# Computing the shift of an adaptive layer norm with four 128x32 column tiles of TensorE and a VectorE transpose

## The chip, the cores and the metric

The kernel runs on one core of a Trainium2 chip. The metric is the device time of one execution in microseconds; a kernel's time is the median of several executions. TensorE multiplies matrices (its stationary operand is loaded by a separate instruction, shown as PEld), VectorE (DVE) and ScalarE (ACT) do element-wise work, GpSimd (POOL) does a few reductions and small operations, and SyncE (SP) issues nearly all DMA transfers.

## The reference, cut to what matters

```python
B, N, D = (2, 256, 1152)          # all inputs bfloat16

def reference(x, c, wqkv, wo, w_mod):
    mod = (_silu(c) @ w_mod).reshape(B, 6, 1, D)
    shift_a, scale_a, gate_a, ... = [mod[:, i] for i in range(6)]
    h = _layernorm(x, axis=-1) * (1 + scale_a) + shift_a
    qkv = h @ wqkv                 # split into q, k, v of D columns each
    p = _softmax(jnp.einsum('bqd,bkd->bqk', q, k) * D ** (-0.5), axis=-1)
    a = jnp.einsum('bqk,bkd->bqd', p, v) @ wo
    return x + gate_a * a
```

Each batch has one shift, one scale and one gate vector of 1152 values. They are products of `_silu(c)`, a matrix of 2 rows, with slices of `w_mod`.

## The kernel before, in words

The 512 tokens of both batches form one token axis (T = 512). The 1152 features are KT = 9 slices of 128. Nearly everything is kept with features on the partitions and tokens along the free axis, so that `xnT`, `hTs` and `hT` are tiles of 128 x 9 x 512.

Every instruction goes through a small recorder (class `_Rec`, line 65), and at the end `pin` ties the instructions of each engine to the order in which the program wrote them. So the order of the source lines is the order on every engine. Because of the recorder the profile gives line 74 for nearly all instructions, and groups are told apart by the names of their tiles.

The stages are, in order of time:

1. Loads, statistics of the layer norm, transposition of the centred x into `xnT`, and the scale vectors (`psS0`, `psSA`, `psM`, `psL`), which become `s1p` = 1 + scale.
2. The K projection without shift: `hTs` = `xnT` x `s1p`, and accumulation over the nine feature slices. Six of the nine blocks of 128 K columns are accumulated side by side in six PSUM banks (`accs`, NACC = 6). Of the next two (NEARLY = 2) the first KA = 3 slices are computed early and put into the SBUF tile `early`; the other six slices follow later in `k_block`, and VectorE adds the two parts into `qkT`. The ninth block comes last. (A shift of K adds the same number to all scores of a query, which the softmax takes out, and so K does without it.)
3. The shift. `shift_block(kk)` (lines 312 to 317) issues nine matmuls for the kk-th part of the contraction. Their stationary operand is a 128x128 block of `wH`, the shift's slice of `w_mod`. Their moving operand is `sc_rhs(kk)`: silu(c) for both batches, repeated to NR = 54 columns. The result has features on the partitions; `psH` is 128 x 9 x 54, of which two columns of each slice are copied to `sh`. On TensorE four such groups of nine stand ahead of the blocks 6 and 7 of K, one between them, and four behind. The last K block follows (lines 472 to 475).
4. `modulated(i)` computes `hT` = `xnT` x `s1p` + `sh` for 18 pieces (nine slices, two batches); every third goes to ScalarE, the others to VectorE.
5. Nine q blocks of nine matmuls each (lines 510 to 518) read `hT` slice by slice, from `chunks_w`, and ScalarE evacuates them into `qkT`. Then come the scores, the softmax, the value blocks, the products with the probabilities and the output projection. While TensorE does the q blocks, VectorE accumulates the gate vectors (`gacc`), 18 steps of 1152 columns.

PSUM has six banks that rotate (pool `psum`, tag `mm`) and two single ones (`psum_a`, tag `pa`; `psum_b`, tag `pb`). In SBUF the pools lie one behind the other in the order in which they are opened: `const` (small tiles, `sh` among them), `wpool` (`wK` and the q and v weights), `act`, `small`, `work`, and later `wmpool` (`wS`, `wH`).

All loads are issued by SyncE in the order of the program; `wH` is loaded in five parts behind the K weights, and the first q weights follow.

Of the kernel before, what the change touches and what calls it, by code (L numbers as in the profile page):

```python
# [8 lines left out]
ALU = mybir.AluOpType  # L9
AX = mybir.AxisListType  # L10
F32 = mybir.dt.float32
BF16 = mybir.dt.bfloat16
# [4 lines left out]
def kernel(  # L17
# [10 lines left out]
    P = 128  # L28
    B, N, D = x.shape
    T = B * N  # L30
    KT = D // P
    TT = T // P
    NQ = N // P
    CW = 384
# [4 lines left out]
    NACC = 6  # L39
    NEARLY = 2  # L40
    WE = (NACC + NEARLY) * P
    KA = 3
    KM = 2 * KA
    NR = 54
# [4 lines left out]
    wmod_v = w_mod.rearrange("(p kk) (s n) -> p kk s n", p=P, s=6)  # L49
    wo_v = wo.rearrange("(k p) n -> p k n", p=P)  # L50

    const = ctx.enter_context(tc.tile_pool(name="const", bufs=1))
    wpool = ctx.enter_context(tc.tile_pool(name="wpool", bufs=1))
    act = ctx.enter_context(tc.tile_pool(name="act", bufs=1))
    small = ctx.enter_context(tc.tile_pool(name="small", bufs=4))
    work = ctx.enter_context(tc.tile_pool(name="work", bufs=2))
    psum = ctx.enter_context(tc.tile_pool(name="psum", bufs=6, space=PSUM))
    psum_a = ctx.enter_context(tc.tile_pool(name="psum_a", bufs=1, space=PSUM))
    psum_b = ctx.enter_context(tc.tile_pool(name="psum_b", bufs=1, space=PSUM))
# [21 lines left out]
    vec = _Rec(nc.vector, dve_seq)  # L81
    sca = _Rec(nc.scalar, act_seq)
    ten = _Rec(nc.tensor, pe_seq)
# [12 lines left out]
    def tok(b):  # L96
        return slice(b * N, (b + 1) * N)
# [4 lines left out]
        out=ident, in_=ident, compare_op=ALU.not_equal, fill=1.0, base=0,  # L102
# [14 lines left out]
        out=pick, in_=pick, compare_op=ALU.is_ge, fill=0.0, base=0,  # L117
# [3 lines left out]
        out=pick, in_=pick, compare_op=ALU.is_ge, fill=0.0, base=NT - 1,  # L121
# [10 lines left out]
    wK = wpool.tile([P, KT, D], BF16)  # L132
    chunk_cols = [vc * CW for vc in range(NCH)] + [2 * D + vc * CW for vc in range(NCH)]
    chunks_w = [wpool.tile([P, KT, CW], BF16, tag=f"wchunk{i}", name="wqv") for i in range(2 * NCH)]
    wmpool = ctx.enter_context(tc.tile_pool(name="wmpool", bufs=1))
    wS = wmpool.tile([P, KT, D], BF16, tag="wS")
    wH = wmpool.tile([P, KT, D], BF16, tag="wH")

# [62 lines left out]
    def sc_rhs(kk):  # L201
        return scT_rep[:, kk].rearrange("p r b -> p (r b)")
# [5 lines left out]
    hT = act.tile([P, KT, T], BF16)  # L208
# [62 lines left out]
    def rstd_spread():  # L271
# [4 lines left out]


    s1p = const.tile([P, KT, B], F32)
    sh = const.tile([P, KT, B], F32)
    hTs = act.tile([P, KT, T], BF16, tag="a3")  # L280
    qkT = act.tile([P, 2 * KT, T], BF16)
    early = const.tile([P, NEARLY, T], F32)
# [3 lines left out]
               rhs=ones_row[0:1, 0 : (KA - 1) * NR], start=True, stop=False, skip_group_check=True)  # L286
    psS0 = psum_b.tile([P, NR], F32, tag="pb")
    ten.matmul(psS0, lhsT=ones_bf[0:1, :], rhs=ones_row[0:1, 0:NR], start=True, stop=False,
               skip_group_check=True)
# [19 lines left out]
            for b in range(B):  # L309
                scaled(k, tok(b), s1p[:, k, b : b + 1])  # L310

    def shift_block(kk):
        for j in range(KT):
            ten.matmul(
                psH[:, j, :], lhsT=wH[:, kk, j * P : (j + 1) * P], rhs=sc_rhs(kk),
                start=(kk == 0 and j == 0), stop=(kk == KT - 1), skip_group_check=True,
            )

    def one(t):
# [26 lines left out]
    def k_block(f, ps, k0):  # L346
        for k in range(k0, KT):
            ten.matmul(
                ps, lhsT=wK[:, k, f * P : (f + 1) * P], rhs=hTs[:, k, :],
                start=(k == k0), stop=(k == KT - 1),  # L350
            )

    def evac(idx, out_ap, in_ap):
        if idx % 2 == 0:
            return vec.tensor_copy(out=out_ap, in_=in_ap)
        return sca.copy(out=out_ap, in_=in_ap)
# [100 lines left out]
        k_step(k)  # L457
    for f in range(NACC):
        evac(1, qkT[:, KT + f, :], accs[f])
    psH = psum_a.tile([P, KT, NR], F32, tag="pa")  # L460
    for kk in range(4):
        shift_block(kk)
    for i in range(NEARLY):
        pool, tag = (psum_b, "pb") if i == 0 else (psum, "mm")
        ps = pool.tile([P, T], F32, tag=tag, name="ps")
        k_block(NACC + i, ps, KA)
        vec.tensor_tensor(out=qkT[:, KT + NACC + i, :], in0=ps, in1=early[:, i, :], op=ALU.add)
        shift_block(4 + i)
    for kk in range(4 + NEARLY, KT):
        shift_block(kk)  # L470
    vec.tensor_copy(out=sh, in_=psH[:, :, 0:B])
    for f in range(NACC + NEARLY, KT):
        ps = psum.tile([P, T], F32, tag="mm")
        k_block(f, ps, 0)
# [2 lines left out]
    def modulated(i):  # L477
        k, b = divmod(i, B)
        if i % 3 == 2:
            sca.activation(  # L480
                out=hT[:, k, tok(b)], in_=xnT[:, k, tok(b)], func=ACT.Identity,
                bias=sh[:, k, b : b + 1], scale=s1p[:, k, b : b + 1],
            )
        else:
            vec.tensor_scalar(
                out=hT[:, k, tok(b)], in0=xnT[:, k, tok(b)],
                scalar1=s1p[:, k, b : b + 1], scalar2=sh[:, k, b : b + 1],
                op0=ALU.mult, op1=ALU.add,
            )

    for i in range(KT * B):
        modulated(i)
    evac(1, qkT[:, 2 * KT - 1, :], last_k)


# [11 lines left out]
        spq.dma_start(out=wO[:, k0 : k0 + 3, :], in_=wo_v[:, k0 : k0 + 3, :])  # L507


    for f in range(KT):  # L510
        wt, off = chunks_w[f * P // CW], f * P % CW
        ps = psum.tile([P, T], F32, tag="mm")
        for k in range(KT):
            ten.matmul(
                ps, lhsT=wt[:, k, off : off + P], rhs=hT[:, k, :],
                start=(k == 0), stop=(k == KT - 1),
            )
        evac(1, qkT[:, f, :], ps)


    s_tiles = []
    for b in range(B):
        s_ps = psum.tile([P, NQ, N], F32, tag="mm")
        for i in range(NQ):
            tq = b * NQ + i
            for k in range(KT):
                ten.matmul(
                    s_ps[:, i, :],
                    lhsT=qkT[:, k, tq * P : (tq + 1) * P],
                    rhs=qkT[:, KT + k, tok(b)],  # L530
                    start=(k == 0), stop=(k == KT - 1),
# [96 lines left out]
    for b in range(B):  # L628
        for gi, dv0 in enumerate(range(0, KT, 2)):
            ndv = min(2, KT - dv0)  # L630
            ps = psum.tile([P, 2, N], F32, tag="mm")
            for dd in range(ndv):
                dv = dv0 + dd
                for j in range(NQ):
                    ten.matmul(
                        ps[:, dd, :], lhsT=v_sb[:, b * NQ + j, dv * P : (dv + 1) * P], rhs=pT_sbs[b][:, j, :],
                        start=(j == 0), stop=(j == NQ - 1),
# [3 lines left out]
    for t in range(TT):  # L641
# [9 lines left out]
        for ci, (c0, w_) in enumerate(chunks):  # L651
# [3 lines left out]
            ps = psum.tile([P, w_], F32, tag="mm")  # L655
            if pregated:
                ten.matmul(ps, lhsT=ident, rhs=x_sb[:, t, cs], start=True, stop=False)
            for k in range(KT):
                ten.matmul(
                    ps, lhsT=attnT[:, k, t * P : (t + 1) * P],  # L660
                    rhs=(wo_last[:, k, c0 - (D - TAILW) : c0 - (D - TAILW) + w_] if pregated else wO[:, k, cs]),
                    start=(k == 0 and not pregated), stop=(k == KT - 1),
# [49 lines left out]
```

## Time and profile before

| | us |
|---|---|
| median of 3 runs | 97.81 (97.72 to 98.03) |
| the profiled execution, its own time | 98.07 |
| its span, first to last instruction | 96.2 |
| TensorE busy | 90.3 |
| VectorE busy | 70.4 |
| ScalarE busy | 33.7 |
| the 81 shift matmuls, first to last start | 26.1 to 30.8 |

The span is what the views of the trace show; the time around it (98.07 - 96.2 = 1.87 us) lies before the first and behind the last instruction. A timeline line gives start, length, engine, operation, output and inputs, the number of instructions merged, and in brackets the idle time before them with what ended it. Matmuls overlap: the length of one is its latency, and the distance between two starts is what a stream of them costs. The granted clock of TensorE was 1.000 over the whole span.

### The profile page before, as it was taken

What the parts mean: (1) busy time and instruction counts of PE and PEld (TensorE: products, weight loads), DVE (VectorE), ACT (ScalarE), POOL (GpSimd) and SP (SyncE); (2) the same over time, 40 slices, a digit from 0 to 9 for tenths busy, and PEclk for the clock granted to TensorE, in tenths of its full rate; (3) what the DMA queues carried; (4) which work ended last, traced back from release to release, by engine and by line L of the source; (5) the groups of instructions that cost most, each with busy time, mean ns of one, the idle gap of its engine ahead of it and who ended that gap; (6) DMA issues with size and microseconds to landing.
All of it is one profiled execution on the core that took longest, in us unless ns stands there. A gap on an engine that the chain in (4) does not pass through costs nothing.

```text
span 96.2 us, 1820 instructions
## 1 busy us (share of the span) xinstructions
PE 90.3 (94%) x722; PEld 55.4 (58%) x727; DVE 70.4 (73%) x138; ACT 33.7 (35%) x68; POOL 21.4 (22%) x26
## 2 busy tenths in 40 slices
PE   5968799999999999999999999999999999999980
PEld 1338599553566444444448756665568756665670
DVE  0398669224999999999992999991228677998880
ACT  5198577201570972342222436332115400000010
POOL 6600000820000000000000000007999980016000
PEclk9999999999999999999999999999999999999999
DMA  1999999999999999999999502110000000303131
GB/s 33 332 357 372 324 384 376 397 393 416 390 378 396 384 410 387 374 373 372 387 410 408 201 0 48 37 24 0 0 0 0 7 0 0 123 0 123 67 120 58
DMA packets 19015, 21.31 MB, mean 221 GB/s; under 512 B 2752, under 2 KB 13632, under 8 KB 19008
## 3 DMA queue, kind: packets, MB, share of 16 engines
q1 hardware_dynamic: 18592, 21.16, 61.3%
q10 hardware_dynamic: 416, 0.05, 0.3%
q8 instruction: 5, 0.08, 0.3%
q14 instruction: 2, 0.02, 0.0%
HBM read 19.76 MB, written 1.18 MB: 218 GB/s over the span
## 4 chain that ended last, share of the span: by engine, by line
PE 84%; DMA 10%; SPq 2%; issue 1%; DVE 1%; ACT 0%
PE ps L74 63%; PE acc L74 11%; DMA wK<-in_wqkv_dram 5%; DMA wS<-in_w_mod_dram 4%; PE s_ps L74 4%; PE psH L74 2%; SPq L74 2%; PE psE L74 1%; PE psL L74 1%; PE tp L74 1%; DVE xnT L74 0%; PE spread_ps L74 0%; DVE hTs L74 0%; ACT o_sb L74 0%; PE turn_ps L74 0%
## 5 line engine op out<-in xcount | busy, mean ns | idle before, releaser
L74 POOL PARTITION_ALL_REDUCE gate_bc<-gacc x2 | 13.7, 6886 | 45.5 <-DVE gacc L74 45.5
L74 DVE SCALAR_TENSOR_TENSOR gacc<-wG,scT_f,gacc 128x1152 f32<-128x1152 bf16 x16 | 22.7, 1418 | 0.5
L74 PE MATMUL ps<-wqv,hT 128*128 128x384 bf16 x108 | 17.7, 326 | 0.0
L74 PE MATMUL ps<-hT,wqv 128*128 128x512 bf16 x80 | 17.6, 379 | 0.1
L74 PE MATMUL ps<-wO,attnT 128*128 128x384 bf16 (+1 forms) x108 | 17.0, 319 | 0.0
L74 PEld LDWEIGHTS <-attnT 128*128 128x128 bf16 x126 | 11.4, 98 | 6.3
L74 PEld LDWEIGHTS <-hT 128*128 128x128 bf16 x108 | 10.6, 98 | 6.9
L74 PE MATMUL acc<-hTs,wK 128*128 128x128 bf16 (+2 forms) x88 | 13.2, 292 | 1.1 <-DMA wK<-in_wqkv_dram 0.6
L74 PEld LDWEIGHTS <-wK 128*128 128x128 bf16 x123 | 9.9, 97 | 6.8 <-DMA wK<-in_wqkv_dram 0.9
L74 PEld LDWEIGHTS <-wqv 128*128 128x128 bf16 x81 | 7.9, 98 | 9.6 <-DVE hT L74 0.4
L74 ACT CAST qkT<-ps 128x512 bf16<-128x512 f32 x10 | 5.8, 583 | 10.9 <-PE ps L74 10.9
L74 DVE TENSOR_TENSOR ga<-ps,gate_bc 128x384 f32<-128x384 f32 (+1 forms) x12 | 6.5, 538 | 2.7 <-PE ps L74 2.7
L74 ACT CAST v_sb<-ps 128x384 bf16<-128x384 f32 x10 | 4.7, 476 | 9.8 <-PE ps L74 9.8
L74 DVE TENSOR_TENSOR o_sb<-ga,x_sb 128x384 bf16<-128x384 f32 (+1 forms) x12 | 6.8, 565 | 0.4
L74 DVE TENSOR_TENSOR xnT<-xnT,rstd_bc 128x512 bf16<-128x512 bf16 x9 | 5.5, 686 | 1.6 <-ACT rstd_bc L74 1.6
L74 ACT CAST o_sb<-ps 128x128 bf16<-128x128 f32 (+1 forms) x2 | 0.5, 238 | 17.0 <-PE ps L74 17.0
L74 PE MATMUL junk_ps<-junk_rhs 128*128 128x512 bf16 x13 | 4.7, 540 | 1.1 <-DVE junk_rhs L74 1.1
L74 DVE BATCH_NORM_STATS2 stats<-x_sb 128x6 f32<-128x384 bf16 x6 | 3.1, 551 | 2.8 <-DMA x_sb<-in_x_dram 2.8
L74 PE MATMUL ps<-hTs,wK 128*128 128x512 bf16 x19 | 4.7, 378 | 0.1
L74 DVE CAST attnT<-ps 128x512 bf16<-128x512 f32 (+1 forms) x6 | 3.5, 603 | 1.7 <-PE ps L74 1.7
L74 DVE CAST v_sb<-ps 128x384 bf16<-128x384 f32 x2 | 1.1, 558 | 4.6 <-PE ps L74 4.6
L74 DVE TENSOR_SCALAR hTs<-xnT,s1p 128x256 bf16<-128x256 bf16 (+1 forms) x20 | 4.2, 272 | 0.1
(82 smaller groups left out, 89.8 us busy)
## 6 DMA issues: line engine op xcount, KB each, us to landing
wqv<-in_wqkv_dram SPq DMA_DIRECT2D x5, 864.0 KB, 10.1
wG<-in_w_mod_dram SPq DMA_DIRECT2D x3, 864.0 KB, 9.6
wO<-in_wo_dram SPq DMA_DIRECT2D x3, 864.0 KB, 8.5
wH<-in_w_mod_dram SPq DMA_DIRECT2D x4, 576.0 KB, 7.4
wS<-in_w_mod_dram SPq DMA_DIRECT2D x6, 288.0 KB, 6.2
wK<-in_wqkv_dram SPq DMA_DIRECT2D x6, 288.0 KB, 6.4
x_sb<-in_x_dram SPq DMA_DIRECT2D x4, 288.0 KB, 3.6
wqv<-in_wqkv_dram SPq DMA_DIRECT2D x3, 288.0 KB, 8.6
```

The costliest lines, as they stand in the source:

```text
L74: r = fn(*a, **k)
```

## The change

The shift's operands change places. The stationary operand is now 32 columns of silu(c) (16 repetitions of the two batches), the moving operand 288 columns of `wH`: for column group j, columns 32j to 32j + 31 of each of the nine slices. The four groups use the four 128x32 column tiles of TensorE and write partitions 32j to 32j + 31 of `psH`. So 36 matmuls take the place of 81. The result has batches on the partitions; VectorE's transpose of 32x32 blocks turns it, all 288 columns, into `sh`, which is 128 x 9 x 32 now.

The K blocks 6 and 7 run ahead of the shift and stay in their PSUM banks ("parked"); their additions come behind the 18 modulations. The first two q blocks are computed in turns, slice by slice, in two banks.

The pools are opened in another order: a lead tile of 128 bytes, `wpool`, `act`, `wmpool`, `work`, and behind them `const` and `small`.

```diff
-    const = ctx.enter_context(tc.tile_pool(name="const", bufs=1))
+    lead = ctx.enter_context(tc.tile_pool(name="lead", bufs=1))
+    lead.tile([P, 64], BF16, name="lead")
     wpool = ctx.enter_context(tc.tile_pool(name="wpool", bufs=1))
     act = ctx.enter_context(tc.tile_pool(name="act", bufs=1))
+    wmpool = ctx.enter_context(tc.tile_pool(name="wmpool", bufs=1))
+    work = ctx.enter_context(tc.tile_pool(name="work", bufs=2))
+    const = ctx.enter_context(tc.tile_pool(name="const", bufs=1))
     small = ctx.enter_context(tc.tile_pool(name="small", bufs=4))
-    work = ctx.enter_context(tc.tile_pool(name="work", bufs=2))
...
-    sh = const.tile([P, KT, B], F32)
+    sh = const.tile([P, KT, 32], F32)
...
-    def shift_block(kk):
-        for j in range(KT):
+    def shift_rows(kk):
+        w4 = wH[:, kk, :].rearrange("p (f j c) -> p f j c", j=4, c=32)
+        for j in range(4):
             ten.matmul(
-                psH[:, j, :], lhsT=wH[:, kk, j * P : (j + 1) * P], rhs=sc_rhs(kk),
-                start=(kk == 0 and j == 0), stop=(kk == KT - 1), skip_group_check=True,
+                psH[32 * j : 32 * (j + 1), :, :], lhsT=sc_rhs(kk)[:, 0:32], rhs=w4[:, :, j, :],
+                start=(kk == 0), stop=(kk == KT - 1), skip_group_check=True, tile_position=(0, 32 * j),
             )
...
-    psH = psum_a.tile([P, KT, NR], F32, tag="pa")
-    for kk in range(4):
-        shift_block(kk)
+    parked = []
     for i in range(NEARLY):
         pool, tag = (psum_b, "pb") if i == 0 else (psum, "mm")
-        ps = pool.tile([P, T], F32, tag=tag, name="ps")
-        k_block(NACC + i, ps, KA)
-        vec.tensor_tensor(out=qkT[:, KT + NACC + i, :], in0=ps, in1=early[:, i, :], op=ALU.add)
-        shift_block(4 + i)
-    for kk in range(4 + NEARLY, KT):
-        shift_block(kk)
-    vec.tensor_copy(out=sh, in_=psH[:, :, 0:B])
+        parked.append(pool.tile([P, T], F32, tag=tag, name="ps"))
+        k_block(NACC + i, parked[i], KA)
+    psH = psum_a.tile([P, KT, 32], F32, tag="pa")
+    for kk in range(KT):
+        shift_rows(kk)
+    vec.transpose(out=sh.rearrange("p f r -> p (f r)"), in_=psH.rearrange("p f r -> p (f r)"))
...
     for i in range(KT * B):
         modulated(i)
+    for i in range(NEARLY):
+        vec.tensor_tensor(out=qkT[:, KT + NACC + i, :], in0=parked[i], in1=early[:, i, :], op=ALU.add)
     evac(1, qkT[:, 2 * KT - 1, :], last_k)
...
-    for f in range(KT):
-        wt, off = chunks_w[f * P // CW], f * P % CW
-        ps = psum.tile([P, T], F32, tag="mm")
+    for fs in ((0, 1), *((f,) for f in range(2, KT))):
+        pss = [psum.tile([P, T], F32, tag="mm", name="ps") for _ in fs]
         for k in range(KT):
-            ten.matmul(
-                ps, lhsT=wt[:, k, off : off + P], rhs=hT[:, k, :],
-                start=(k == 0), stop=(k == KT - 1),
-            )
-        evac(1, qkT[:, f, :], ps)
+            for f, ps in zip(fs, pss):
+                wt, off = chunks_w[f * P // CW], f * P % CW
+                ten.matmul(
+                    ps, lhsT=wt[:, k, off : off + P], rhs=hT[:, k, :],
+                    start=(k == 0), stop=(k == KT - 1),
+                )
+        for f, ps in zip(fs, pss):
+            evac(1, qkT[:, f, :], ps)
```

More of the change, by code (lines that the diff above doesn't have):

```diff
@@ L134 @@
     chunks_w = [wpool.tile([P, KT, CW], BF16, tag=f"wchunk{i}", name="wqv") for i in range(2 * NCH)]
-    wmpool = ctx.enter_context(tc.tile_pool(name="wmpool", bufs=1))
     wS = wmpool.tile([P, KT, D], BF16, tag="wS")
```

## The prediction

> **What bounds the kernel now.** I read the page first, then the chain of waits in order of time, then the timeline of each engine around the edit, then the transfers' times to landing.
>
> ```profile
> span 96.2 us, 1820 instructions
> PE 90.3 (94%) x722; PEld 55.4 (58%) x727; DVE 70.4 (73%) x138; ACT 33.7 (35%) x68; POOL 21.4 (22%) x26
> ```
>
> TensorE is busy for 94% of the span. The chain says where that sets the end (start, length, what):
>
> ```profile
> 23.61 2.70 PE acc L74 x12
> 26.30 0.91 PE psH L74 x36
> 27.21 0.06 issue
> 27.27 1.24 PE ps L74 x5
> 28.51 0.23 PE psH L74 x9
> 28.73 1.29 PE ps L74 x6
> 30.03 0.91 PE psH L74 x36
> 30.94 0.22 PE ps L74
> 31.16 0.05 issue
> 31.21 10.74 PE ps L74 x49
> ...
> 50.37 3.93 PE s_ps L74 x36
> 54.30 39.17 PE ps L74 x272
> ```
>
> From 23.61 us to the last matmul nothing but TensorE stands in the chain. The shift's 81 matmuls are three of its pieces, so what they cost less, the end moves forward, unless another wait takes the place. The candidates are VectorE and the transfers. VectorE around the edit:
>
> ```profile
> 24.26 5.51 DVE L74 TENSOR_TENSOR xnT<-xnT,rstd_bc 128x512 bf16<-128x512 bf16 x9 [1.56 <-ACT rstd_bc L74]
> 29.69 1.28 DVE L74 TENSOR_TENSOR qkT<-ps,early 128x512 bf16<-128x512 f32 x2
> 30.98 0.18 DVE L74 COPY sh<-psH 128x18 f32<-128x18 f32 x1
> 31.19 3.17 DVE L74 TENSOR_SCALAR hT<-xnT,s1p,sh 128x256 bf16<-128x256 bf16 x12
> 34.28 0.81 DVE L74 TENSOR_SCALAR gacc<-wG,scT_f 128x1152 f32<-128x1152 bf16 x1
> 52.37 0.69 DVE L74 TENSOR_TENSOR p_f<-s_ps,rstd_bc 128x512 f32<-128x512 f32 x1 [2.01 <-PE s_ps L74]
> ```
>
> VectorE runs without a pause from 24.26 us, and has 2.01 us to spare when it reaches the first softmax step at 52.37.
>
> **The change part by part.**
>
> *Removed: 81 matmuls.* The chain's pieces psH are 0.91 + 0.23 + 0.91 = 2.05 us, or 25 ns for each matmul of 54 columns. All of it is on the path.
>
> *Added: 36 matmuls of 288 columns, four beside each other.* The pitch of wide matmuls comes from the timeline: the q blocks start at 32.72 us and the scores at 50.20, with 81 matmuls of 512 columns between, so 17.48 / 81 = 0.2158 us for 512 columns, and 288 columns are 0.1214 us. A step kk has four of them. If the four column tiles stream together, nine steps are 9 x 0.1214 = 1.09 us, and the last of the four starts three issue slots later, 3 x 0.025 = 0.08. If they stream one after another, 36 x 0.1214 = 4.37 us. No row of before shows two column tiles in flight. One row shows one tile of that shape (12 stationary columns, in a tile of 32), with its neighbours:
>
> ```profile
> 21.36 0.38 PE L74 MATMUL acc<-hTs,wK 128*128 128x512 bf16 x1
> 21.67 0.22 PE L74 MATMUL turn_ps<-ident,parts 128*12 128x128 bf16 x1
> 21.82 0.60 PE L74 MATMUL acc<-hTs,wK 128*128 128x512 bf16 x2
> ```
>
> It starts 0.31 us after its predecessor where 0.216 is usual (0.09 lost), and its successor 0.15 us after it where 128 columns need 0.054 (0.10 lost): entering and leaving the narrow tile costs 0.19 us. The new block enters and leaves once.
>
> *Which end I take.* Bounds for the block: below, 36 issue slots of 25 ns, 0.91 us with free edges; above, 4.37 + 0.19 = 4.56 us. I take the concurrent case, 1.09 + 0.08 + 0.19 = 1.36 us. The nearest rows are the psH matmuls themselves: each lasts 185 ns but a new one starts every 25 ns, weight load included, so four loads and starts (0.10 us) fit into one 0.1214 us stream; and the four tiles write different partitions of psH and use different columns of the array. Gain: 2.05 - 1.36 = 0.69 us.
>
> The Trainium skill bears on both halves. "TensorEngine Tiling (Array Packing)", section Key Properties, says a change of tiling mode drains TensorE; the 0.09 and 0.10 us above agree. "TensorE: Matmul & The Clock Gate", Part 3 (Measured speedup vs the span model), gives 2.38 times for three column tiles instead of 3; at that efficiency four would need 4.37 / 3.17 + 0.19 = 1.57 us (an estimate from that page) and the gain would be 0.48 us. No run here shows it yet.
>
> *Moved: the two blocks of K columns 6 and 7 now run ahead of the shift* (12 matmuls, 2.59 us, no change in number). They start at 26.14 us, the block of the shift at 26.14 + 2.59 = 28.73 and K block 8 at 28.73 + 1.36 = 30.09, against 30.78 before (timeline; the chain gives 30.94, the end of the last shift matmul). wH's five transfers were issued from 16.6 to 20.1 us and took 6.7 to 8.5 us, so the last had landed by 28.6: the shift waits for none.
>
> *Evacuation of the shift: COPY of 18 columns (0.18 us) becomes a transpose of 288.* No row is a transpose. Bounds: 0.18 us, and 0.69 us for a 512-column read of PSUM (p_f row); by width between the two, 0.18 + 0.51 x 270 / 494 = 0.46. VectorE is free of the nine multiplications at 29.77, the last shift matmul ends about 30.2, so sh stands at 30.66 and hT starts at 30.70 against 31.19: 0.49 earlier. TensorE reaches the q blocks 1.94 us after 30.09, at 32.03, and the first hT pair is done at 31.3. Even at 0.69 us, or a half microsecond more, the transpose is covered by K block 8.
>
> *q blocks 0 and 1 take turns.* Same 18 matmuls, no cost. Alone, block 0 would want the last slice of hT at 32.03 + 8 x 0.216 = 33.76, when VectorE finishes it (30.70 + 3.17 = 33.87); taking turns it is wanted at 35.48. So it prevents a stall of 0.1 to 0.3 us, and none existed before (80 q matmuls in 17.65 us leave no hole).
>
> *The two additions for K columns 6 and 7 (1.20 us at their spacing, 29.69 to 30.98 less the pause) go behind the modulation.* Queued behind them are the gate's accumulations: these start at 30.70 + 3.08 + 1.20 = 34.98 instead of 34.28, 0.70 later. The eleven others keep their pace (wG's later parts land before they are wanted: issue 26.8 and 30.1, 10.8 and 9.6 us to landing, wanted about 38.7 and 43). VectorE reaches the softmax 0.70 later and TensorE's scores are 0.69 earlier: of the 2.01 us of slack, 0.62 is left. Without that cover the delay would be small still: the value blocks occupy TensorE to 71.7 us while the turned probabilities were there at 63.6. The parked PSUM banks are wanted again only by q block 5.
>
> *Transfers.* No DMA is added or moved. The q weights' second and third parts land at 35.4 and 42.1 (issue 25.7 and 30.9, plus 9.7 and 11.2); q blocks 3 and 6 want them at 37.9 and 43.7, so an earlier TensorE still finds them.
>
> *Pools.* wK starts at byte 40,704 of a partition before and 16,640 after, both multiples of 256; so do all other weight and activation tiles, because the grown sh (1,152 bytes instead of 72) now lies behind them. Small tiles moved from 0 to 32 beyond a multiple of 64. I take nothing for it; the bound is the stretch in which TensorE waits for transfers, 2.65 to 11.94 us: 3% either way would be 0.3 us.
>
> **The sum.** The profiled execution took 98.07 us, of which the span is 96.2: 98.07 - 0.69 = 97.38. It lay 0.26 above the median of the runs; from the median 97.81, 97.12 us.
>
> **Rivals.**
> - *The four tiles stream one after another.* The block is 4.56 us, 2.51 more than before; nothing hides it, as everything behind waits for sh or for TensorE: 97.81 + 2.51 = 100.32 us. It turns slower once the block passes 2.05 us. For it: no row shows two tiles together. Against: different columns and partitions. 0.07.
> - *Weight loads set the pace.* The narrow tile's load took 0.08 us in the trace; four in a row per step are 0.32 us, and 9 x 0.32 + 0.19 = 3.07: +1.02, 98.83 us. For it: each matmul has its own load, and a load after a change of tile was not pulled ahead (0.42 us of idle before it). Against: loads at full width keep to the 25 ns pitch. 0.11. In one sentence from the skill: the Tiling page (Restrictions) says column tiling switches the fast weight load off, which would feed this rival.
> - *Half of the overlap.* Pace 0.2 us a step, through the moving operand's runs of 32 columns out of 128 or loads partly shown: 9 x 0.2 + 0.19 = 2.0, no change, 97.8 us. 0.11.
> - *The wait moves to VectorE* (transpose or additions): covered by the slacks above, so only with a transpose over 1.2 us, 0.02, at about 97.7.
>
> **Chances and range.** Forecast 0.69, the rivals 0.07, 0.11, 0.11 and 0.02. About 0.3% (0.29 us) is what a measurement of this kernel can tell from no change. The forecast's own range is 96.8 (block near 1.1 us) to 97.5 (the estimate with four at the lower efficiency, and the pools); the half overlap reaches 98.2. Faster 0.68, within 0.12, slower 0.20. To leave out no more than 2 in 10 the range goes from 96.6 to 98.3.
>
> **What would show it.** Right: psH matmuls in groups of four starting about 0.12 us apart per step; the block from 28.7 to 30.1; hT from about 30.7; q blocks from 32.0 without a hole; VectorE's wait before p_f about 0.6 us. Wrong: steps of 0.2 us or more, a hole ahead of the q blocks, or a first stage (to 11.9 us) of another length.

## The result and the profile after

The changed kernel takes 97.0 us (median of 15 runs, 96.35 to 98.28), the kernel before 97.81 (15 runs, 97.04 to 98.21). The ratio is 0.9916 with a 95% interval of 0.9886 to 0.9945: faster by 0.8%, or 0.81 us of the medians. The profiled execution of after took 97.0 us, of which 95.2 are the span.

The page of after, its first two parts:

```profile
span 95.2 us, 1731 instructions
PE 90.8 (95%) x678; PEld 54.6 (57%) x682; DVE 70.6 (74%) x138; ACT 33.5 (35%) x68; POOL 21.4 (22%) x26
```

The chain of waits of after (start, length, what):

```profile
23.33 2.69 PE acc L78 x12
26.02 2.59 PE ps L78 x12
28.61 1.22 PE psH L78 x36
29.83 0.32 PE ps L78
30.15 0.05 issue
30.20 10.74 PE ps L78 x49
...
49.36 3.93 PE s_ps L78 x36
53.29 39.17 PE ps L78 x272
```

Three pieces of psH, 2.05 us, have become one of 1.22, and everything behind them is as long as it was: 3.93 us of scores and 39.17 us of the rest in both kernels. VectorE in the timeline of after, from two windows:

```profile
25.80 3.69 DVE L78 TENSOR_TENSOR xnT<-xnT,rstd_bc 128x512 bf16<-128x512 bf16 x6
29.88 0.48 DVE L78 STREAM_TRANSPOSE sh<-psH 128x288 f32<-128x288 f32 x1 [0.40 <-PE psH L78]
30.40 3.16 DVE L78 TENSOR_SCALAR hT<-xnT,s1p,sh 128x256 bf16<-128x256 bf16 x12
33.48 1.28 DVE L78 TENSOR_TENSOR qkT<-ps,early 128x512 bf16<-128x512 f32 x2
34.68 0.81 DVE L78 TENSOR_SCALAR gacc<-wG,scT_f 128x1152 f32<-128x1152 bf16 x1
```
```profile
51.36 0.69 DVE L78 TENSOR_TENSOR p_f<-s_ps,rstd_bc 128x512 f32<-128x512 f32 x1 [0.60 <-PE s_ps L78]
```

The transpose takes 0.48 us where the copy took 0.18, but now VectorE waits 0.40 us for TensorE ahead of it. The slack ahead of the softmax has shrunk from 2.01 to 0.60 us.

**Where to measure.** The stage ahead of the edit is the same code in both kernels, and yet it did not end at the same time: the first matmul behind the six accumulators started at 26.14 us in the profile of before and at 25.86 in that of after. Over the profiles of all kernels below it lies between 25.33 and 26.80 us, without order. So the 1.0 us between the two spans is not all the edit's. What the edit does is read from the *tail*: from the start of the last accumulating matmul plus its pace of 0.216 us, which is where the next one starts in both kernels, to the end of the last matmul. Before: 26.14 to 93.46, 67.32 us. After: 25.86 to 92.45, 66.59 us. The edit is worth 0.73 us there; the 0.81 of the medians agrees within its interval. The tail repeats well: 66.59 us again in a second profile of after, 67.32 in that of a kernel with before's instructions.

### The profile page after: what moved, and what is told of

The parts are those of the page before. It is cut to its first block, busy times and chain, and to the rows that moved or that the text cites. A ratio compares the mean times of both kernels' runs of the same rounds, so it can differ in the third digit from the quotient of the medians.

```text
span 95.2 us, 1731 instructions
## 1 busy us (share of the span) xinstructions
PE 90.8 (95%) x678; PEld 54.6 (57%) x682; DVE 70.6 (74%) x138; ACT 33.5 (35%) x68; POOL 21.4 (22%) x26
## 4 chain that ended last, share of the span: by engine, by line
PE 95%; DVE 1%; issue 0%; ACT 0%
PE ps L78 64%; PE acc L78 13%; PE junk_ps L78 6%; PE s_ps L78 4%; PE tp L78 2%; PE psE L78 1%; PE psH L78 1%; PE psL L78 1%; PE psM L78 1%; PE psSA L78 1%; PE psS L78 0%; PE spread_ps L78 0%; DVE hTs L78 0%; ACT o_sb L78 0%; DVE junk_rhs L78 0%
## 5 line engine op out<-in xcount | busy, mean ns | idle before, releaser
L78 PE MATMUL junk_ps<-junk_rhs 128*128 128x512 bf16 x13 | 5.7, 630 | 1.1 <-DVE junk_rhs L78 1.1
```

Of the source, the lines that this page charges most:

```text
L78: r = fn(*a, **k)
```

## The experiments

All ran beside the kernel before on one chip per group (e0 and e2 to e4; e1 and e5 to e7; f1 to f4), so the ratios are comparable within a group. "Tail" is as above, from one profile each.

| kernel | median us | ratio to before (95%) | tail us |
|---|---|---|---|
| before | 97.81 | 1 | 67.32 |
| change | 97.0 | 0.9916 (0.9886 to 0.9945) | 66.59 |
| e0, change again | 97.07 | 0.9932 (0.9904 to 0.9961) | 66.59 |
| e1, tile by tile | 98.86 | 1.0107 (1.0067 to 1.0147) | 68.47 |
| e2, pools in the old order | 98.63 | 1.0067 (1.0036 to 1.0098) | 67.85 |
| e3, before with the new pools | 97.73 | 1.0011 (0.9982 to 1.0041) | 67.32 |
| e4, shift in three blocks | 97.56 | 0.9979 (0.9949 to 1.0009) | 67.03 |
| e5, q blocks in a row | 96.93 | 0.9912 (0.9886 to 0.9938) | 66.78 |
| e6, additions first | 97.25 | 0.9932 (0.9905 to 0.9959) | 66.74 |
| e7, both of these | 98.02 | 1.0017 (0.9987 to 1.0046) | 67.50 |
| f1, before shifted by 32 bytes | 98.59 | 1.0079 (1.0049 to 1.011) | 67.74 |
| f2, e2 at 64 bytes | 98.35 | 1.0068 (1.0044 to 1.0093) | 67.79 |
| f3, e2 at 128 bytes | 98.06 | 1.0059 (1.003 to 1.0089) | 67.22 |
| f4, e2 with q weights first | 97.24 | 0.9966 (0.994 to 0.9991) | 66.59 |

**e0, the yardstick.** No edit.

> The changed kernel once more, as the yardstick for the others on one chip. My account (the shift's block on TensorE shrinks from 2.05 to about 1.3 us, everything behind it moves forward by that): 0.7 us under before, ratio 0.993, block of the shift 1.3 us, q blocks start about 5.85 us after the first matmul of K block 6. Rival (the first stage, which ended 0.28 us earlier in the one profile of after, belongs to the gain): 1.0 us under before, ratio 0.990, with the first K-block-6 matmul again near 25.9 us instead of 26.1.

The ratio came out at 0.9932, and the q blocks start 5.86 us after the first matmul of K block 6. The tail is 66.59 us again, but it began at 26.80. So the earlier start in the first profile of after did not come back, and nothing here speaks for the rival.

**e1, the order of the tiles.**

```diff
-    for kk in range(KT):
-        shift_rows(kk)
+    for j in range(4):
+        for kk in range(KT):
+            shift_rows(kk, j)
```

> The change with the same 36 matmuls in another order: nine for the first column tile, then nine for the second, and so on. My account (what makes the block short is that neighbours in the order go to different tiles): one after another, 36 x 0.1214 + 0.19 = 4.56 us instead of 1.3, everything behind 3.2 us later: 100.2 us. Rival (fewer instructions are what helps, 36 for 81, or TensorE overlaps tiles whatever the order): block 1.3 to 1.6 us, 97.0 to 97.3 us.

TensorE's timeline of after in a window that ends at 28.6 us, and that of this run in a window from 28.0 to 28.5 us:

```profile
28.23 0.38 PE L78 MATMUL ps<-hTs,wK 128*128 128x512 bf16 x1
28.54 0.31 PE L78 MATMUL psH<-wH,scT_rep 128*32 128x288 bf16 x4
```
```profile
27.66 0.59 PE L78 MATMUL ps<-hTs,wK 128*128 128x512 bf16 x2
28.18 0.54 PE L78 MATMUL psH<-wH,scT_rep 128*32 128x288 bf16 x3
```

In after four matmuls have started by then (3 ns apart by their records), and they last 0.31 us together, hardly more than one, whose length is 0.286 to 0.296. In the other order three have started after 0.32 us, 0.12 apart. The chain of this run:

```profile
25.66 2.59 PE ps L78 x12
28.25 3.09 PE psH L78 x36
31.35 19.53 PE ps L78 x90
```

The same 36 instructions take 3.09 us instead of 1.22, the tail is longer than that of the change by about as much, 1.88 us, and the kernel is slower than before by 1.1%. So the gain comes from neighbours in the order that go to different tiles, not from fewer instructions. The size was off: 3.09, not 4.56. In the single starts of the trace the 36 matmuls form four rows of nine, with 0.1225 us from start to start (0.13 to the second of a row). The rows begin at 28.184, 28.812, 29.441 and 30.070 us, each 5 or 6 ns behind the sixth start of the row ahead. The semaphores (the flags that an instruction waits for) in the records tell which tile a row belongs to: only the first tile's nine matmuls wait for the five parts of `wH`, and those that wait for the fourth and the fifth part start at 28.929 and 29.174 us. So the second tile began while three matmuls of the first, which stand ahead of it in the program, had not yet started. That is why the block took 3.09 us and not 4.56; what makes it three is open.

**e4, the price of entering and leaving.** The shift is cut as in the kernel before: four steps ahead of K block 6, one between 6 and 7, four behind.

```diff
+    for kk in range(4):
+        shift_rows(kk)
     for i in range(NEARLY):
...
         k_block(NACC + i, parked[i], KA)
+        if i == 0:
+            shift_rows(4)
-    for kk in range(KT):
+    for kk in range(5, KT):
         shift_rows(kk)
```

> The change with the shift cut into three blocks (four steps, one, four) around the K blocks 6 and 7, as in the kernel before; nothing else differs. My account (entering and leaving the narrow tile costs 0.19 us each time): 2 x 0.19 = 0.38 us over the yardstick, 97.4 us. Rival (the edges cost nothing beyond the stream's own fill, and running the K blocks ahead of the shift is without effect): 97.0 us.

The chain of this run:

```profile
26.29 0.60 PE psH L78 x14
26.89 1.40 PE ps L78 x6
28.29 0.24 PE psH L78 x4
28.53 1.40 PE ps L78 x6
29.93 0.60 PE psH L78 x16
```

Each piece pays its own edges: 0.60 + 0.24 + 0.60 = 1.44 us against 1.22 in one piece, and the six K matmuls behind the first and the second take 1.40 us where 6 x 0.2158 = 1.29 is their pace. The tail is longer by 0.44: 0.22 us for each further pair of edges, where 0.19 was expected. The ratio is higher by 0.0047, about as much, though the intervals of the two ratios overlap.

**e5, e6, e7: the covers.**

```diff
-    for fs in ((0, 1), *((f,) for f in range(2, KT))):
+    for fs in ((f,) for f in range(KT)):
```

is e5; e6 has the two additions into `qkT` ahead of the shift and its transpose; e7 has both.

> The change with q blocks 0 and 1 one after the other, as in the kernel before. My account (the last slice of hT is ready at about the moment at which q block 0 alone would want it): a stall of 0 to 0.3 us in q block 0, 97.0 to 97.3 us; by the profile of after the last hT piece ends 1.59 us after q begins and q block 0 would want it 1.73 us after, so rather 0 to 0.1. Rival (the turns carry the gain): 0.5 us or more.

> The change with the two additions of the parked blocks ahead of the transpose on VectorE, as in the kernel before; q blocks 0 and 1 still take turns. My account: the second parked block is done at about 28.6 us, so the additions end near 30.6 to 30.7, the transpose starts 0.8 us later and hT 0.8 us later, at 31.2; q begins at 31.7 and wants its slices in turns of 0.43 us, which the 0.35 us per slice of VectorE and ScalarE keep ahead of, apart from the first: 0 to 0.15 us over the yardstick. Rival (the place of the additions carries the gain): 0.6 to 0.8 us over it.

> The change with both undone: additions ahead of the transpose, q blocks one after the other. My account (each of the two covers for the other; without both, q block 0 runs into hT): the last hT piece ends about 2.4 us after q begins, wanted 1.73 us after: a stall of 0.6 to 0.8 us, 97.7 us, all of the gain gone. Rival (neither matters): 97.0 us.

Against 66.59 us the tails are longer by 0.19 (e5), 0.15 (e6) and 0.91 us (e7). The small two do not show in the medians. In e5 the stall is more than the 0 to 0.1 us of my account, which had read the profile of after wrongly: there the last piece of `hT` ends 1.85 us after q begins, not 1.59 (there the last but one of VectorE ends). The third is more than the 0.6 to 0.8 expected: the q blocks begin 0.15 us later, and block 0 loses 0.76 us inside. It takes the whole gain, and its chain no longer runs through TensorE alone:

```profile
23.52 0.59 ACT rstd_bc L78
24.11 0.02 issue
24.14 5.51 DVE xnT L78 x9
29.64 1.20 DVE qkT L78 x2
30.84 0.40 DVE sh L78
31.24 0.03 issue
31.27 2.66 DVE hT L78 x10
33.93 0.04 issue
33.98 16.45 PE ps L78 x75
```

VectorE is the chain from 24.14 to 33.93 us: the multiplications, the additions, the transpose and ten pieces of `hT`, and q block 0 waits for slice after slice. Either of the two moves alone gives VectorE nearly enough room; without both, the time won on TensorE is spent on waiting.

**e2 and e3: the pools.** e2 opens the pools in the order of before (the reverse of that part of the change's diff); because `sh` is larger, all weights and activations then start 32 bytes beyond a multiple of 256. e3 is the kernel before with the new order and nothing else.

> The change with the pools in the order of before, so that the grown sh pushes all weights and activations to 32 bytes beyond a multiple of 256. My account (places in SBUF cost nothing): the same as the yardstick, 97.0 to 97.1 us. Rival (starts off a multiple of 256 slow the transfers or the reads): a transfer rate some per cent lower in the stretch up to 50 us and a first stage 0.3 us or more longer; 97.4 us and up.

> The kernel before with the pools of the changed kernel and nothing else. My account: the time of before, 97.8 us. Rival (the new places are worth the 0.28 us that the first stage was shorter by): 97.5 us.

The new order alone does nothing (e3, tail 67.32). But without it the change is slower than before. A window from 12 to 40 us of after and of e2 (busy time of PE, PEld, DVE, ACT, POOL, then clock, DMA share and GB/s):

```profile
12.00:40.00 28.00, 27.82 (x244) 15.32 (x245) 21.84 (x57) 13.07 (x27) 2.54 (x8) 1.00 1.06 389
```
```profile
12.00:40.00 28.00, 27.76 (x241) 15.10 (x243) 20.61 (x55) 12.85 (x25) 2.53 (x8) 1.00 1.08 366
```

The DMA engines are as busy and move 6% less: packets of 768 bytes (rows of 384 numbers) take 40.4 ns instead of 36.6 on average, those of 2,304 bytes (rows of 1152) 100.9 instead of 95.1. So my account of e2 fell, and the rival's slower transfers came, but not its longer first stage: the tail of this profile began at 25.54 us. The chain of e2 shows where TensorE notices:

```profile
31.89 12.36 DMA wqv<-in_wqkv_dram
44.26 0.05 issue
44.30 6.00 PE ps L76 x27
50.30 3.93 PE s_ps L76 x36
```

The third part of the q weights lands at 44.26 us; q block 6 would have begun at 31.61 + 54 x 0.2158 = 43.26 and loses 1.03. Another 0.20 us is lost in the shift, whose last step waits for wH. Of the 1.26 us that the tail is longer, 1.23 are these two waits. In after the same part landed at 42.72 and was wanted at 43.37: 0.65 us to spare.

**f1 to f4: is it the start address, and only through this wait?** f1 is the kernel before with a tile of 32 bytes more in `const`; f2 and f3 are e2 with 32 and 96 bytes more (starts 64 and 128 bytes beyond a multiple of 256); f4 is e2 with the last part of the gate's weights issued behind the third part of the q weights (a line of `load_mod` moved down):

```diff
         if i == 1:
             load_mod(wG, 2, 3, 6, 0, D)
+        if i == 2:
             load_mod(wG, 2, 6, KT, 0, D)
```

> The kernel before with one more tile of 32 bytes in const, so that weights and activations start 32 bytes beyond a multiple of 256; nothing else differs. My account after the run with the old pools (such starts make the transfers some 6% slower, 768-byte packets 40 ns instead of 36, and TensorE pays only where it catches up with them, at q block 6): before reaches q block 6 at 44.4 us and its weights land at about 44.2, so a stall of 0 to 0.3 us, 97.8 to 98.2 us, although the transfers run at about 366 GB/s instead of 391. Rival (the places slow the engines' own reads, or cost their 1.2 us in any kernel): 99 us.

> The change with the old order of the pools and 32 bytes more in const: weights and activations start 64 bytes beyond a multiple of 256. Theory A (any start off a multiple of 256 costs): 768-byte packets take 40 ns, q block 6 waits about 1 us, 98.6 us. Theory B (only starts off a multiple of 64 cost): packets take 36 ns, no wait, 97.0 us.

> The same with 96 bytes more in const: starts 128 bytes beyond a multiple of 256. Theory A (any start off a multiple of 256 costs): 98.6 us. Theory B (multiples of 64, or of 128, are enough): 97.0 us, packets of 768 bytes 36 ns.

> The change with the old order of the pools (32 bytes off), and the last part of the gate's weights loaded behind the third part of the q weights instead of ahead of it. My account (of the 1.26 us that the old pools cost, 1.03 are the wait of q block 6 for the third part of the q weights, which lands 1 us too late): that part lands some 2.3 us earlier, the wait is gone, and of the 1.26 us about 0.2 are left: 97.3 us; VectorE gets the gate's weights later, which its slack and that of the value blocks cover. Rival (the slower transfers cost elsewhere too, or the wait moves to the gate): 98.2 us or more.

The chain of f1, in which nothing but the start addresses differs from before:

```profile
32.04 12.38 DMA wqv<-in_wqkv_dram
44.42 0.05 issue
44.46 6.00 PE ps L74 x27
```

The packets of 768 bytes took 40.5, 39.9, 40.0 and 40.2 ns on average, and the rate from 12 to 40 us was 365, 367, 367 and 362 GB/s: a start at 64 or 128 is as bad as one at 32, which is theory A. q block 6 lost 0.41, 1.02 and 0.62 us in f1 to f3 (distance of its first matmul to the one ahead, less 0.216), as the third part of the weights landed at 44.42, 45.19 and 44.25. In f4, with the transfers as slow as in e2, it landed at 42.46 and the wait is gone:

```profile
26.48 2.59 PE ps L76 x12
29.07 1.22 PE psH L76 x36
30.29 19.53 PE ps L76 x90
```

Its tail is 66.59 us, that of after. So from the accumulators on, slow transfers cost nothing but waits for a part that lands too late. Two sizes were missed: f1 lost 0.77 us by its ratio where 0 to 0.3 was expected, and its tail explains 0.42; and f4 stays 0.0034 above e0's ratio, with the same tail. What is left, 0.35 and 0.33 us, the tails do not explain, and its cause stays open. For f4 it need not be real: the intervals of the two ratios overlap, and they come from different groups. For f1 the traces offer a reading: in the four profiles in which q block 6 waits (e2, f1, f2, f3), the span is 51.89 to 51.90 us longer than the landing time of the third part, whenever TensorE got there. So an execution in which that part lands later is longer by as much, and the profiled one of f1 (98.12 us) was faster than its median by 0.47.

No version here beats the change by more than the measurement can tell.

## Why the prediction was right

**The time.** Forecast 97.12 us from the median of before; measured 97.0.

**The block.** Forecast 1.36 us and a gain of 0.69; measured from the first narrow matmul's usual place (28.45) to the first matmul of K block 8 (29.76): 1.31 us, and 0.73 in the tail. Nine steps of 0.1225 us, against 0.1214 from the pitch of wide matmuls; the three further tiles of a step start 3 ns apart, not 25; entering cost 0.09 and leaving 0.12 us, forecast 0.19 together from the one narrow matmul of before. The concurrency, which no row of before showed, was the chosen end, and e1 shows that it is what the gain hangs on. It was an argued choice between two bounds until then.

The Trainium skill's efficiency (TensorE: Matmul & The Clock Gate, Part 3, 2.38 times for three tiles) was too low for this case: 36 x 0.1225 = 4.41 us of stream ran in 9 x 0.1225 = 1.10, four times. The Trainium skill's rule that a change of tiling mode drains TensorE (TensorEngine Tiling (Array Packing), Key Properties) agrees with the 0.22 us a pair in e4.

**The rivals.** One after another: e1 made that happen in part, and the change then loses, though less than that rival's price (3.09 us for the block instead of 4.56). Weight loads as the pace, and half of the overlap: fell with steps of 0.1225 us.

**The transpose, hT and the turns.** Forecast 0.46 us for the transpose, measured 0.483. From the first matmul behind the accumulators to hT: 5.05 us before, 4.54 after, 0.51 earlier where 0.49 was forecast. The stall that the turns prevent: forecast 0.1 to 0.3 us, 0.19 in e5. (The parked bank of K block 7 is wanted by q block 4, not 5; the additions end at 34.76 us and that block starts at 39.48, so nothing hangs on it.) The slack ahead of the softmax: forecast 0.62, measured 0.60.

**What was sized wrongly: the transfers and the pools.** I gave the third part of the q weights about 1.5 us to spare (42.1 against 43.7); it had 0.65, as the transfers of that execution ran 0.57 us later and TensorE started its tail earlier, and only 0.44 in e0 (landed 43.87, wanted 44.31). So the margin that kept this wait away was thinner than forecast, and that it held is in part luck. And I took nothing for the pools, with a bound in the first stage. For what the change does that is right (e3). But the cover should have been named with its price: the start at a multiple of 256 hides a wait of 1.03 us at q block 6 and 0.20 in the shift, and without it the change would have been slower than before (e2). The Trainium skill has such a rule, told of reads: a descriptor that doesn't start at a multiple of 256 bytes costs extra, because its first transaction starts at the boundary below (DMA: Bandwidth & Descriptors, How a descriptor splits into AXI transactions). Here it is the SBUF side, which is written, that moved, and the packets took 10% (768 bytes) and 6% (2,304 bytes) longer; whether it is for that reason no run here shows.

## What to carry to other kernels

A product with two live rows need not send its large operand through the weight loads: as moving operand in four column tiles it took 1.31 us instead of 2.05, provided that neighbours in the order go to different tiles and the block is entered once. When a block on TensorE shrinks, look at what VectorE and the transfers owe it next; here three small moves (parked additions, two q blocks in turns, pools in another order) kept the gain, and undoing the first two, or the third, took all of it. A tile that grows by a few bytes moves all that lies behind it; check the start addresses of the tiles that transfers write.

## What the runs showed of the hardware

- Transfers into tiles that start 32, 64 or 128 bytes beyond a multiple of 256 ran at 362 to 367 GB/s from 12 to 40 us (five profiles), those into tiles at multiples of 256 at 388 to 393 (nine profiles).
- Four 128x32 tiles in turns ran at the pace of one: their matmuls started 3 ns apart, and a step took 0.1225 us, where one stream of 288 columns takes 0.1214 by the pitch of wide matmuls.
- Matmuls of 128x32 tiles in the order of the tiles did not run strictly one after another: 36 took 3.09 us, though 36 x 0.1225 are 4.41. The first matmul of a tile started ahead of the last three of the tile before it.
- The same instructions ahead of the tail ended between 25.33 and 26.80 us in 14 profiles. For an edit behind them, the length of the tail told 0.2 us apart where the medians did not.
